# New order and new engines for the steps of a planned spectral-filter and ReGLU kernel

## The chip, the cores and the metric

The kernel runs on one core of one Trainium2 chip. The metric is the device time of one execution in microseconds (us), lower is better. A core has five engines that run their own instruction queues side by side: TensorE (PE, matrix products; PEld are its weight loads), VectorE (DVE), ScalarE (ACT), GpSimd (POOL) and SyncE (SP, which issues most DMAs).

## The reference

Everything is float32; x has 2048 rows of 512.

```python
def _A_ref(x, w_r, w_i):
    X = rfft2(x, axes=(-2, -1))
    return irfft2(X * (w_r + 1j * w_i), s=(S, D), axes=(-2, -1))

def _B_ref(x, W_gate, W_up, W_down):          # F = 1376
    gate = einsum("bsd,df->bsf", x, W_gate)
    up = einsum("bsd,df->bsf", x, W_up)
    gate = gate * (gate > 0)
    return einsum("bsf,fd->bsd", gate * up, W_down)

xn = _layernorm(x)
s = _A_ref(xn, A_w_r, A_w_i)
g = silu(_B_ref(xn, B_W_gate, B_W_up, B_W_down))
return x + s * g
```

## The kernel before

**The work.** The rows are held in eight chunks of 256 (two row tiles of 128) for the layernorm and the filter, and in four chunks of 512 (`c` = 0 to 3, four row tiles each) for the feed-forward part. All products are split into a high and a low float16 half and taken in three passes (high by high, high by low, low by high).

- *Filter.* The two-dimensional transform is done by matrix products. A first stage writes chunk after chunk to the DRAM buffer `A_d`. Then eight column groups `q` go through four PE stages each, `y`, `xx`, `z`, `v`, between which DVE and ACT build halves (`a`, `xsp`, `tt`, `pf`, `p`, `z`, `t`); the filter weights come in at `tt` (four products of 128x512 each group), and `pf` are their sums. The result goes to `C_d`. When all eight are there, a last stage per row chunk (`s`) gives `zz`, from which sums and differences `ae`, `ye` and `sv` are made; `sv` is the filtered signal.
- *Feed-forward.* For each row chunk and each of eleven feature tiles (ten of 128 and one, tile 10, of 96), `gu` are the gate and up products, `r` the rectified gate, `h` the product, in its float16 halves. `dn` is the down product, `g` its Silu. `rows_mw` is one small product that spreads a maximum over the partitions, from `wide_mw`, which DVE makes out of `mw`.
- *Nine pairs.* In row chunks 2 and 3, nine pairs of feature tiles (four in chunk 2, five in chunk 3) are computed by `fast_products` with seven block products of 12 matmuls instead of eight. The PE accumulates into three PSUM tiles `sa`, `sb`, `sc`; the other names are `sk` (a copy of `sc`), `se`, `sr`, `sq` and then two `h`. Such a pair needs sums of weight blocks: `rp` (four steps of 128x512 for a pair, one after the other), out of which `wT` and a part of `wgu` are made.
- *End.* `finish` multiplies `sv` by `g` (chunks before the last come back from the DRAM buffer `G_d`), adds x and stores. For some chunks x is copied to the output first and `sv` is added by a DMA that POOL issues; for the others DVE adds into `xt` and SP stores.

**What sets the order.** Nothing is issued when it is written. Each piece of work is a step with an engine, a cost, the tiles that it reads and writes, and a due time. `Plan.run` goes through all steps with a model of the five engines; each time it takes the step that can begin soonest, and among those that can begin equally soon the one that is due first. The planned start times give one list, and each engine executes its part of that list in this order; a helper records every instruction, so that all lines of the profile are its line, L197 (L206 after the change). `DUES` holds a due time for every step, and `WAITS` holds, for the steps that have one, how long before its due time a step may begin at the earliest:

```python
for s, due in zip(steps, DUES):
    s.due = due
for s, lead in zip([s for s in steps if s.lead is not None], WAITS):
    s.lead = lead
...
order.sort(key=lambda k: k[0])
for t, s in order:
    s.fn()
```

Other tables choose the engine of single steps: `NORMS` (normalising a row tile, DVE or ACT), `SUM2` (the sums `pf` or `tt`, two choices for each column group), `DIFF2` (the differences `ae`, two for each row chunk), `TSUMS` (the four `rp` steps of a pair), `SECONDS` (the product `se<-se,sq` of a pair) and `HLOWS` (the low half of a pair's `h`, two for each pair). `ROOM` holds the number of buffers of each kind; it is not changed, and for most `dn` tiles there is one PSUM buffer.

```python
eng, e, cost = (DVE, "DVE", dve(512)) if TSUMS[n] == "DVE" else (POOL, "POOL", pool(512))
e, eng, cost = (("DVE", DVE, dve), ("POOL", POOL, pool))[SECONDS[5 * c + n] == "POOL"]
e, eng, cost = (("DVE", DVE, dve), ("POOL", POOL, pool))[HLOWS[10 * c + 2 * n + m] == "POOL"]
```

Of the kernel before, what the change touches and what calls it, by code (L numbers as in the profile page):

```python
# [43 lines left out]
NORMS = ['DVE', 'DVE', 'DVE', 'DVE', 'DVE', 'ACT', 'ACT', 'DVE', 'DVE', 'DVE', 'ACT', 'DVE', 'DVE', 'ACT', 'DVE', 'DVE']  # L44
STATS, ADDS, COPIES = ['DVE', 'DVE', 'ACT', 'DVE', 'ACT', 'ACT', 'ACT', 'ACT'], ['DMA', 'DMA', 'DVE', 'DMA', 'DMA', 'DMA', 'DVE', 'DVE'], [105.83, 202.31, 0.24, 342.73, 748.16, 416.58, 501.03, 895.66]
# [9 lines left out]
SUM2, DIFF2 = ['DVE', 'DVE', 'DVE', 'POOL', 'POOL', 'DVE', 'DVE', 'POOL', 'DVE', 'POOL', 'DVE', 'POOL', 'DVE', 'POOL', 'DVE', 'POOL'], ['POOL', 'POOL', 'POOL', 'POOL', 'POOL', 'POOL', 'DVE', 'DVE', 'DVE', 'POOL', 'DVE', 'DVE', 'DVE', 'POOL', 'POOL', 'DVE']  # L55
ROOM = {"k4": 10, "k2": 8, "kg": 4, "cm": 3, "h16": 11, "xg": 3, "F": 2, "gu": 3, "dn": 1, "q": 4, "q4": 2, "mv": 4, "m": 4, "p": 4, "am": 1, "mid": 3}
CALM, SAFE, SAFE_LAG, RATE, TURNKB = 40, 1.0, 1.0, 320, 1300
SUMS, TSUMS, FMARGIN = ['DVE', 'DVE', 'DVE', 'DVE'], ['DVE', 'DVE', 'DVE', 'DVE', 'DVE'], 0.4
SECONDS, HLOWS = ['DVE', 'DVE', 'DVE', 'DVE', 'DVE', 'DVE', 'DVE', 'DVE', 'DVE', 'DVE', 'DVE', 'DVE', 'DVE', 'DVE', 'DVE', 'DVE', 'DVE', 'DVE', 'DVE', 'DVE'], ['DVE', 'DVE', 'DVE', 'DVE', 'DVE', 'DVE', 'DVE', 'DVE', 'DVE', 'DVE', 'DVE', 'DVE', 'DVE', 'DVE', 'DVE', 'DVE', 'DVE', 'DVE', 'DVE', 'DVE', 'DVE', 'DVE', 'DVE', 'DVE', 'DVE', 'DVE', 'DVE', 'DVE', 'DVE', 'DVE', 'DVE', 'DVE', 'DVE', 'DVE', 'DVE', 'DVE', 'DVE', 'DVE', 'DVE', 'DVE']
# [4 lines left out]
XDUE, SDUE = [-44.18, 1.62, 81.91, 105.7, 173.95, 99.44, 177.4, 146.02], [-114.62, 32.24, 147.09, 211.35]  # L64
DUES = (
    61.11, 143.08, 138.41, 136.86, 1e+09, 1e+09, 1e+09, 1e+09, 1e+09, 1e+09, 1e+09, 1e+09, 1e+09, 1e+09, 1e+09, 1e+09, 1e+09, 1e+09, 1e+09, 1e+09,
    1e+09, 1e+09, 1e+09, 1e+09, 1e+09, 1e+09, 1e+09, 1e+09, 1e+09, 1e+09, 1e+09, 1e+09, 1e+09, 1e+09, 1e+09, 1e+09, 1e+09, 1e+09, 1e+09, 1e+09, 1e+09,
    1e+09, 1e+09, 1e+09, 1e+09, 1e+09, -207.26, -219.43, -107.81, -43.91, -59.59, -32.12, -41.62, -126.94, -114.77, -112.31, -30.63, -43.52, -40.73,
# [1501 lines left out]
```

## Time and profile before

| | |
|---|---|
| median of 3 runs | 407.5 us (406.91 to 407.97) |
| the profiled execution | 408.49 us, its span 406.7 us |
| granted TensorE clock | 0.994 (1.00 from 170 to 400 us) |
| busy: PE, DVE, ACT, POOL | 391.2, 339.0, 245.4, 30.8 us |
| instructions on PE, DVE, ACT, POOL | 3332, 755, 478, 50 |
| first matmul, last matmul's end | 1.06 us, about 398.5 us |

The span runs from the first to the last instruction of the profiled execution; its own time is 1.8 us longer. PE's busy time counts a matmul as busy until the next one may follow, so a wait of PE shows as a gap between the starts of two matmuls and as an idle time in square brackets in the timeline, with what ended it. The other engines' idle time matters only where PE or the end waits for them.

### The profile page before, as it was taken

The numbers are of one execution on the slowest core, as the hardware profiler recorded it, in microseconds if no ns is written. First come the engines' busy times: TensorE is split into PE (matmuls) and PEld (weight loads), VectorE is DVE, ScalarE is ACT, GpSimd is POOL, SyncE is SP. The second block draws the span as 40 slices with busy tenths as digits, with TensorE's granted clock in tenths as the row PEclk, the third lists the DMA queues.
The fourth block names the chain that finished last, engine by engine and source line by source line (L and its number), as shares of the span: only waits on it lengthen the run. The fifth ranks groups of instructions, "written<-read, shape, count | busy, mean of one in ns | idle before, by whom it ended". The sixth has DMA issues, their size and how long they took to land.

```text
span 406.7 us, 8600 instructions
## 1 busy us (share of the span) xinstructions
PE 391.2 (96%) x3332; PEld 242.9 (60%) x3332; DVE 339.0 (83%) x755; ACT 245.4 (60%) x478; POOL 30.8 (8%) x50
## 2 busy tenths in 40 slices
PE   7999999999999999999999999999999999989991
PEld 5864444444444444455675776875567888866551
DVE  3899999899889995798787999998788853787993
ACT  5999976778376848664465983445354543662321
POOL 0000000000000000001001000100111000252311
PEclk9999999999999999999999999999999999999997
DMA  7974013049803997999475950545724059947786
GB/s 265 407 265 119 0 54 103 2 87 216 284 15 71 333 326 246 294 201 270 119 232 143 299 134 24 168 86 185 206 64 140 2 146 239 262 57 212 210 201 155
DMA packets 59353, 69.55 MB, mean 171 GB/s; under 512 B 24688, under 2 KB 36560, under 8 KB 59312
## 3 DMA queue, kind: packets, MB, share of 16 engines
q1 hardware_dynamic: 57872, 66.38, 56.1%
q0 software_dynamic: 1440, 2.62, 4.1%
q8 instruction: 26, 0.43, 0.4%
q14 instruction: 15, 0.12, 0.1%
HBM read 43.81 MB, written 22.56 MB: 163 GB/s over the span
## 4 chain that ended last, share of the span: by engine, by line
PE 59%; DVE 17%; DMA 12%; ACT 5%; issue 2%; SPq 2%; POOL 0%; DVEq 0%; ACTq 0%
PE dn L197 17%; PE gu L197 13%; PE sb L197 7%; PE sc L197 5%; PE sa L197 5%; DVE h L197 3%; DMA A_d<-t 3%; PE z L197 3%; PE xx L197 3%; DVE xs L197 2%; SPq L197 2%; PE y L197 2%; DVE t L197 2%; DMA x<-in_x 2%; DMA out<-sv 2%
## 5 line engine op out<-in xcount | busy, mean ns | idle before, releaser
L197 PEld LDWEIGHTS <-wgu 128*128 128x128 f16 x960 | 93.0, 98 | 64.8 <-issue 3.9
L197 PE MATMUL dn<-wds,h 128*128 128x512 f16 (+2 forms) x528 | 118.0, 373 | 1.4 <-ACT g L197 1.4
L197 PE MATMUL gu<-xT,wgu 128*128 128x512 f16 (+1 forms) x528 | 111.9, 369 | 0.4 <-DVE xT L197 0.4
L197 PEld LDWEIGHTS <-h 128*128 128x128 f16 (+1 forms) x594 | 53.8, 98 | 56.1 <-issue 4.6
L197 PEld LDWEIGHTS <-wT 128*128 128x128 f16 x324 | 31.3, 98 | 6.0 <-issue 0.5
L197 POOL TENSOR_TENSOR pf<-tt,tt 128x256 f32<-128x256 f32 x12 | 10.1, 846 | 264.2 <-ACT xsp L197 184.3
L197 PE MATMUL sa<-xT,wgu 128*128 128x256 f16 x216 | 26.6, 273 | 0.0
L197 PE MATMUL sb<-xS,wT 128*128 128x256 f16 x216 | 26.6, 273 | 0.0
L197 ACT ACTIVATE h<-h 128x512 f16<-128x512 f32 (+1 forms) x26 | 16.1, 624 | 15.4 <-DVE h L197 15.3
L197 DVE SCALAR_TENSOR_TENSOR tt<-xsp,cw,wt 128x512 f32<-128x512 f32 x32 | 23.2, 760 | 0.1
L197 DVE TENSOR_TENSOR h<-gu,r 128x512 f32<-128x512 f32 (+3 forms) x34 | 20.7, 608 | 1.8 <-ACT r L197 1.0
L197 ACT ACTIVATE r<-gu 128x512 f32<-128x512 f32 (+2 forms) x26 | 14.9, 574 | 10.8 <-PE gu L197 10.7
L197 DVE TENSOR_TENSOR h<-h,h 128x512 f16<-128x512 f32 (+1 forms) x26 | 17.6, 685 | 2.1 <-ACT h L197 2.0
L197 PE MATMUL gu<-xT,wgt 128*64 128x256 f16 (+1 forms) x144 | 17.1, 309 | 0.5 <-ACT r L197 0.4
L197 ACT ACTIVATE g<-dn,cdi 128x512 f32<-128x512 f32 (+1 forms) x16 | 10.7, 670 | 9.3 <-PE dn L197 5.2
L197 ACT ACTIVATE a<-y 128x1024 f16<-128x1024 f32 x8 | 8.1, 1018 | 12.1 <-PE y L197 11.0
L197 DVE SCALAR_TENSOR_TENSOR wgu<-raw,p,wgu 128x512 f16<-128x512 f32 x20 | 14.2, 746 | 0.1
L197 PE MATMUL sc<-xS,wgu 128*128 128x256 f16 x108 | 13.3, 273 | 0.9 <-DVE sr L197 0.9
L197 PEld LDWEIGHTS <-wgt 128*64 128x64 f16 (+1 forms) x144 | 9.6, 106 | 7.5 <-issue 1.9
L197 POOL TENSOR_TENSOR ae<-zz 128x126 f32<-128x126 f32 (+1 forms) x18 | 10.7, 722 | 40.7 <-issue 37.6
L197 ACT ACTIVATE rp<-rp,csc 128x512 f32<-128x512 f32 x20 | 13.4, 714 | 0.0
L197 PE MATMUL sc<-xT,wT 128*128 128x256 f16 x108 | 13.3, 273 | 0.0
(198 smaller groups left out, 666.2 us busy)
## 6 DMA issues: line engine op xcount, KB each, us to landing
A_d<-t SPq DMA_DIRECT2D x16, 256.0 KB, 4.0
rw<-in_wl SPq DMA_DIRECT2D x8, 512.0 KB, 4.4
wt<-in_wl SPq DMA_DIRECT2D x8, 512.0 KB, 4.9
at<-A_d SPq DMA_DIRECT2D x8, 512.0 KB, 5.3
C_d<-t SPq DMA_DIRECT2D x16, 256.0 KB, 3.5
ct<-C_d SPq DMA_DIRECT2D x16, 256.0 KB, 7.2
x<-in_x SPq DMA_DIRECT2D x7, 512.0 KB, 7.0
G_d<-g SPq DMA_DIRECT2D x12, 256.0 KB, 3.9
```

The lines of the kernel that those rows point to most:

```text
L197: return lambda *args, **kw: self.tc.keep_in_program_order(f(*args, **kw))
```

## The change

All of it is in the tables and in one planner cost. `DUES` and `WAITS` get new numbers, so every engine gets a new order. No instruction is added or taken away but those that two `NORMS` choices bring: PE has the same matmuls. The new choices of engine are:

- two normalisations (`xf<-x,mv,q`) go from DVE to ACT;
- twelve `rp` steps (three of the five pairs), four `se<-se,sq` and seven low halves of `h`, 23 steps of 128x512 in all, go from DVE to POOL;
- eighteen `ae` steps of 128x126 or 128x128 go from POOL to DVE;
- of the sixteen choices for `pf` and `tt` sums seven stay on POOL, but for other groups.

`DEVIATE` replaces a formula for the planner's cost of a DVE step by three constants; it changes no instruction.

```diff
-NORMS = ['DVE', 'DVE', 'DVE', 'DVE', 'DVE', 'ACT', 'ACT', 'DVE', 'DVE', 'DVE', 'ACT', 'DVE', 'DVE', 'ACT', 'DVE', 'DVE']
+NORMS = ['DVE', 'DVE', 'DVE', 'DVE', 'DVE', 'ACT', 'ACT', 'DVE', 'DVE', 'ACT', 'ACT', 'ACT', 'DVE', 'ACT', 'DVE', 'DVE']
-SUM2, DIFF2 = ['DVE', 'DVE', 'DVE', 'POOL', 'POOL', 'DVE', 'DVE', 'POOL', 'DVE', 'POOL', 'DVE', 'POOL', 'DVE', 'POOL', 'DVE', 'POOL'], ['POOL', 'POOL', 'POOL', 'POOL', 'POOL', 'POOL', 'DVE', 'DVE', 'DVE', 'POOL', 'DVE', 'DVE', 'DVE', 'POOL', 'POOL', 'DVE']
+SUM2, DIFF2 = ['DVE', 'POOL', 'DVE', 'POOL', 'DVE', 'POOL', 'DVE', 'POOL', 'POOL', 'DVE', 'POOL', 'DVE', 'DVE', 'POOL', 'DVE', 'DVE'], ['DVE', 'DVE', 'DVE', 'DVE', 'DVE', 'DVE', 'DVE', 'DVE', 'DVE', 'DVE', 'DVE', 'DVE', 'DVE', 'DVE', 'DVE', 'DVE']
-SUMS, TSUMS, FMARGIN = ['DVE', 'DVE', 'DVE', 'DVE'], ['DVE', 'DVE', 'DVE', 'DVE', 'DVE'], 0.4
+SUMS, TSUMS, FMARGIN = ['DVE', 'DVE', 'DVE', 'DVE'], ['POOL', 'DVE', 'POOL', 'POOL', 'DVE'], 0.4
-SECONDS, HLOWS = ['DVE', 'DVE', 'DVE', 'DVE', 'DVE', 'DVE', 'DVE', 'DVE', 'DVE', 'DVE', 'DVE', 'DVE', 'DVE', 'DVE', 'DVE', 'DVE', 'DVE', 'DVE', 'DVE', 'DVE'], ['DVE', 'DVE', 'DVE', 'DVE', 'DVE', 'DVE', 'DVE', 'DVE', 'DVE', 'DVE', 'DVE', 'DVE', 'DVE', 'DVE', 'DVE', 'DVE', 'DVE', 'DVE', 'DVE', 'DVE', 'DVE', 'DVE', 'DVE', 'DVE', 'DVE', 'DVE', 'DVE', 'DVE', 'DVE', 'DVE', 'DVE', 'DVE', 'DVE', 'DVE', 'DVE', 'DVE', 'DVE', 'DVE', 'DVE', 'DVE']
+SECONDS, HLOWS = ['DVE', 'DVE', 'DVE', 'DVE', 'DVE', 'DVE', 'DVE', 'DVE', 'DVE', 'DVE', 'POOL', 'DVE', 'DVE', 'DVE', 'POOL', 'POOL', 'DVE', 'POOL', 'DVE', 'DVE'], ['DVE', 'DVE', 'DVE', 'DVE', 'DVE', 'DVE', 'DVE', 'DVE', 'DVE', 'DVE', 'DVE', 'DVE', 'DVE', 'DVE', 'DVE', 'DVE', 'DVE', 'DVE', 'DVE', 'DVE', 'DVE', 'POOL', 'DVE', 'DVE', 'POOL', 'POOL', 'DVE', 'DVE', 'DVE', 'POOL', 'DVE', 'POOL', 'POOL', 'DVE', 'DVE', 'POOL', 'DVE', 'DVE', 'DVE', 'DVE']
+DEVIATE = (2.68, 2.54, 2.54)
 DUES = (
-    61.11, 143.08, 138.41, 136.86, 1e+09, 1e+09, 1e+09, 1e+09, 1e+09, 1e+09, 1e+09, 1e+09, 1e+09, 1e+09, 1e+09, 1e+09, 1e+09, 1e+09, 1e+09, 1e+09,
+    79.32, 134.5, 138.21, 132.46, 999999978, 999999983, 999999977, 999999984, 999999984, 999999985, 999999984, 999999986, 999999986, 999999987,
...
 )
 WAITS = (
-    44.14, 31.23, 11.27, 23.37, 40.49, 46.88, 145.21, 107.04, 0.1, 22.42, 110.28, 184.68, 43.83, 0.1, 5.2, 82.7, 116.95, 41.45, 22.26, 66.7, 104.78,
+    30.303362, 75.86468, 11.239413, 62.149805, 6.665444, 70.709887, 117.19794, 192.677905, 8.399014, 125.833056, 109.989298, 187.941761, 80.339107,
...
 )
...
-        step("DVE", 2.4 + .14 * sum("ACT" in NORMS[2 * c:2 * c + 2] for c in cs), run, reads=[(f"mv{c}", i) for c in cs for i in range(2 + (STATS[c] == "ACT"))], writes=[(name, 2)], port=True)
+        step("DVE", DEVIATE[cs[0] // 2 - 1], run, reads=[(f"mv{c}", i) for c in cs for i in range(2 + (STATS[c] == "ACT"))], writes=[(name, 2)], port=True)
```

**Where instructions move.** In the rows below the digits of a name are a piece or row tile and a buffer number; the row chunk's digit is cut off.

The first place is DVE around 172 us, where PE needs `wide_mw` for the small product `rows_mw`. `h_1_10` is tile 10's `h` of chunk 1. DVE before:

```order
L197 TENSOR_TENSOR h_1_10_2081<-gu_10_2020,r_10_2067 64x256 x2
L197 TENSOR_TENSOR h_1_10_2081<-gu_10_2020,r_10_2067 32x512
L197 TENSOR_TENSOR h_1_10_2096<-h_1_10_2081,h_1_10_2096 96x512
L197 COPY wt_1950<-spw 128x4 x2
L197 TENSOR_REDUCE mw<-mw 128x1
L197 TENSOR_SCALAR wide_mw<-unit,mw 128x128
```

DVE now, at the same place:

```order
L206 TENSOR_TENSOR sx_3_1_2035<-sx_1_1997,sx_3_1_2035 128x4x256
L206 COPY wt_1926<-spw 128x4 x2
L206 TENSOR_REDUCE mw<-mw 128x1
L206 TENSOR_SCALAR wide_mw<-unit,mw 128x128
L206 TENSOR_TENSOR h_1_10_2110<-gu_10_2041,r_10_2065 64x256 x2
L206 TENSOR_TENSOR h_1_10_2110<-gu_10_2041,r_10_2065 32x512
```

`wide_mw` now stands ahead of tile 10's `h` instead of behind its low half. On PE tile 10's products are parted: the 36 matmuls that stood together are now 12, then three `dn` of 3, and then the other 24 (the up product, 64 columns wide), which wait for ACT's `r`.

The second place is DVE around 220 us, where the pair 0 of chunk 2 ends (`sr_0`) and the sums of column group 2 (`pf`) are made. DVE before:

```order
L197 TENSOR_TENSOR t_0_2783<-v_2751,t_0_2783 128x2x512
L197 TENSOR_TENSOR wT_103<-rp_0_2124,wT_103 128x2x512
L197 TENSOR_TENSOR pf_2823<-tt_2_2749,tt_2_2743 128x8x32
L197 SCALAR_TENSOR_TENSOR tt_2_2826<-xsp_2735,cw,wt_2334 128x512
L197 TENSOR_TENSOR sr_0_2658<-sb_0_2553,sr_0_2658 128x512
L197 TENSOR_TENSOR pf_2823<-tt_2_2826,tt_2_2746 128x8x32
```

DVE now:

```order
L206 TENSOR_TENSOR z_0_2726<-z_2682,z_0_2726 128x1024
L206 SCALAR_TENSOR_TENSOR tt_2_2772<-xsp_2567,cw,wt_2336 128x512
L206 TENSOR_TENSOR tt_2_2772<-tt_2_2772,tt_2_2728 128x256
L206 TENSOR_TENSOR sr_0_2667<-sb_0_2545,sr_0_2667 128x512
L206 SCALAR_TENSOR_TENSOR tt_2_2809<-xsp_2567,cw,wt_2336 128x512
L206 TENSOR_TENSOR tt_2_2745<-tt_2_2745,tt_2_2809 128x256
```

And POOL now, from the sums of weights of one pair (`rp_0_2321`) to those of another (`rp_0_2634`); before, its only rows there were two sums `tt`:

```order
L206 TENSOR_TENSOR rp_0_2321<-rp_0_2321,rp_1_2132 128x512
L206 TENSOR_TENSOR se_0_2676<-se_0_2676,sq_0_2786 128x512
L206 TENSOR_TENSOR pf_2844<-tt_2_2772,tt_2_2728 128x8x32
L206 TENSOR_TENSOR pf_2844<-tt_2_2745,tt_2_2809 128x8x32
L206 TENSOR_TENSOR h_2_0_1_2884<-se_0_2676,h_2_0_1_2884 128x512
L206 TENSOR_TENSOR rp_0_2634<-rp_1_2670,rp_0_2634 128x512
L206 TENSOR_TENSOR rp_1_2670<-rp_1_2670 128x512
```

The sums `pf` are gone from DVE there, and POOL has become the queue in which weight sums, second products, `pf` and low halves of `h` stand behind one another.

The third place is PE around 364 us: the last three matmuls of `dn_2` of chunk 2, and the first of `dn_0` of chunk 3, which takes the same PSUM buffer after ACT has read it for `g`. PE before:

```order
L197 MATMUL dn_2_3886<-wds,h_2_10_3627 128x512
L197 LDWEIGHTS wT_105
L197 MATMUL sb_4_4920<-xS_2966,wT_105 128x256
...
L197 LDWEIGHTS h_3_0_0_4326
L197 MATMUL dn_0_5019<-wds,h_3_0_0_4326 128x512
```

PE now:

```order
L206 MATMUL dn_2_3802<-wds,h_2_10_3684 128x512
L206 LDWEIGHTS wgu_99
L206 MATMUL sb_3_4635<-xS_3019,wgu_99 128x256
...
L206 LDWEIGHTS wgu_100
L206 MATMUL sc_4_4886<-xS_3019,wgu_100 128x256
L206 LDWEIGHTS h_3_0_0_4321
L206 MATMUL dn_0_4905<-wds,h_3_0_0_4321 128x512
```

Before, twelve matmuls (one block product) stand between the two; now it is 36 (`sb`, `sa` and `sc`).

More of the change, by code (lines that the diff above doesn't have):

```diff
@@ L64 @@
 XDUE, SDUE = [-44.18, 1.62, 81.91, 105.7, 173.95, 99.44, 177.4, 146.02], [-114.62, 32.24, 147.09, 211.35]
+DEVIATE = (2.68, 2.54, 2.54)
 DUES = (
-    61.11, 143.08, 138.41, 136.86, 1e+09, 1e+09, 1e+09, 1e+09, 1e+09, 1e+09, 1e+09, 1e+09, 1e+09, 1e+09, 1e+09, 1e+09, 1e+09, 1e+09, 1e+09, 1e+09,
-    1e+09, 1e+09, 1e+09, 1e+09, 1e+09, 1e+09, 1e+09, 1e+09, 1e+09, 1e+09, 1e+09, 1e+09, 1e+09, 1e+09, 1e+09, 1e+09, 1e+09, 1e+09, 1e+09, 1e+09, 1e+09,
-    1e+09, 1e+09, 1e+09, 1e+09, 1e+09, -207.26, -219.43, -107.81, -43.91, -59.59, -32.12, -41.62, -126.94, -114.77, -112.31, -30.63, -43.52, -40.73,
[87 rows of a table removed]
+    79.32, 134.5, 138.21, 132.46, 999999978, 999999983, 999999977, 999999984, 999999984, 999999985, 999999984, 999999986, 999999986, 999999987,
+    999999986, 999999985, 1e+09, 999999989, 999999985, 999999990, 1.00000001e+09, 999999990, 999999994, 999999982, 999999992, 999999991, 999999993,
+    999999996, 999999994, 999999994, 999999975, 999999980, 999999996, 999999996, 999999996, 999999996, 1.00000003e+09, 1.00000004e+09, 999999992,
+    999999998, 999999997, 999999998, 999999999, 999999994, 999999998, 1e+09, -197.42, -228.87, -97.06, -69.59, -51.04, -40.78, -43.63, -76.9, -126.74,
[87 rows of a table added]
 )
 WAITS = (
[12 rows of a table removed]
[19 rows of a table added]
 )
```

203 rows, old and new, of tables (DUES, WAITS) are left out of this document.

## The prediction

> **What bounds the kernel now.** I read the page's parts first, then PE's waits, the 10-us windows, the groups by shape, and the timeline at each wait and at the end.
>
> ```profile
> PE 391.2 (96%) x3332; PEld 242.9 (60%) x3332; DVE 339.0 (83%) x755; ACT 245.4 (60%) x478; POOL 30.8 (8%) x50
> PE   7999999999999999999999999999999999989991
> DVE  3899999899889995798787999998788853787993
> ```
>
> PE is full in nearly every slice, and the change leaves its matmuls alone. So only three things can move the time: places where PE waits, the stretch after the last matmul, and new waits. PE's waits are few (columns: total us, times, longest):
>
> ```profile
> PE gu L197 <- ACT xTf L197: 1.7, 1, 1.7
> PE dn L197 <- ACT g L197: 1.4, 1, 1.4
> PE small L197 <- DVE md L197: 1.1, 1, 1.1
> PE rows_mw L197 <- DVE wide_mw L197: 1.0, 1, 1.0
> PE sc L197 <- DVE sr L197: 0.9, 1, 0.9
> PE gu L197 <- ACT r L197: 0.4, 1, 0.4
> PE gu L197 <- DVE xT L197: 0.4, 1, 0.4
> ```
>
> They sum to 6.9 us. `xTf`, `md` and `xT` belong to the start, whose PE order hardly differs now, and 0.4 for `r` stands between the same steps as before; these I leave. Three remain for the change: 1.4, 1.0 and 0.9, which is 3.3 us.
>
> **The three waits.** The first is at 172 us (start, length, engine, instruction; in brackets the idle time ahead of it):
>
> ```profile
> 172.38 0.69 DVE L197 TENSOR_TENSOR h<-h,h 96x512 f16<-96x512 f32 x1 [0.69 <-ACT h L197]
> 173.62 0.29 DVE L197 TENSOR_SCALAR wide_mw<-unit,mw 128x128 f32<-128x128 f32 x1
> 174.05 0.46 PE L197 MATMUL rows_mw<-wide_mw,ones 128*128 128x128 f32 x2 [0.99 <-DVE wide_mw L197]
> ```
>
> DVE made tile 10's low half, for which it idled 0.69 and worked 0.69, before `wide_mw`. Now `wide_mw` stands ahead of tile 10, and that cover of 1.38 us is larger than the wait of 0.99; PE also has one `dn` of three matmuls more between tile 10's last product and `rows_mw`. What can be late next is what ACT brings into `mw`, and the 24 parted matmuls of tile 10, which newly wait for ACT's `r`. Behind that wait all of PE's queue stands, and DVE's `h` of tile 10. The nearest row is the same pattern in chunk 0, where it costs 0.4 us. I credit 1.0 and debit nothing here; the ends are +0.6 and 0.
>
> The second is at 221 us:
>
> ```profile
> 218.25 2.75 PE L197 MATMUL gu<-xT,wgu 128*128 128x512 f16 x12
> 220.84 1.47 PE L197 MATMUL sa<-xT,wgu 128*128 128x256 f16 x12
> 221.50 0.42 DVE L197 TENSOR_TENSOR pf<-tt,tt 128x256 f32<-128x256 f32 x1 [2.35 <-DMA C_d<-t]
> 222.51 0.69 DVE L197 TENSOR_TENSOR sr<-sb,sr 128x512 f32<-128x512 f32 x1
> 223.25 1.47 PE L197 MATMUL sc<-xS,wgu 128*128 128x256 f16 x12 [0.94 <-DVE sr L197]
> 224.56 2.75 PE L197 MATMUL gu<-xT,wgt 128*128 128x512 f16 x12
> ```
>
> DVE stood 2.35 us in front of `pf` until the store of `t` freed its buffer, and `sr`, which frees the PSUM tile for `sc`, stood behind it in DVE's queue. Now POOL makes `pf`; DVE makes only the `tt` sums there, and the next thing behind `sr` does not hold PE. A wait for that buffer now holds POOL's queue: `se` is ahead of it, the low half of `h` and the next pair's four weight sums are behind it. By starts, twelve matmuls of 256 columns take 224.56 − 223.25 = 1.31 us and twelve of 512 take 220.84 − 218.25 = 2.59. The part of `v` that now stands between, in place of a `gu`, leaves `sr` about 1.5 us to spare by these rows. Credit 0.9.
>
> The third is at 364 us:
>
> ```profile
> 357.63 1.91 POOL L197 DMA_DIRECT2D out<-sv  x2 [1.51 <-DVE sv L197]
> 364.68 0.21 ACT L197 ACTIVATE ye<-zz 128x2 f32<-128x2 f32 x1 [1.94 <-DMA out<-sv]
> 364.79 0.67 ACT L197 ACTIVATE g<-dn,cdi 128x512 f32<-128x512 f32 x1
> 365.51 1.46 PE L197 MATMUL dn<-wds,h 128*128 128x512 f16 x6 [1.44 <-ACT g L197]
> ```
>
> `g` empties the one `dn` buffer, and it stood on ACT behind a two-column copy that waited 1.94 us for the DMA which POOL had issued out of `sv`. Now 36 matmuls (3 × 1.31 = 3.9 us) stand between the two `dn` instead of 12 (1.31), and the copy ahead of `g` waits for DVE's `ae` and no DMA. From rows like these I count `g` done some 2 us after the last `dn_2`, 1.9 ahead of need. Credit 1.4.
>
> **The steps that change engine.** These groups carry the prices (busy us, mean ns):
>
> ```profile
> L197 DVE TENSOR_TENSOR h<-h,h 128x512 f16<-128x512 f32 x22 | 14.9, 685 | 1.4 <-ACT h L197 1.3
> L197 DVE TENSOR_TENSOR ae<-zz 128x128 f32<-128x128 f32 x8 | 2.3, 315 | 0.0
> L197 DVE TENSOR_SCALAR xf<-x,mv,q 128x512 f32<-128x512 f32 x10 | 5.2, 541 | 0.0
> L197 DVE TENSOR_TENSOR p<-pf,p 128x1024 f16<-128x1024 f32 x8 | 10.3, 1288 | 3.3 <-ACT p L197 3.3
> L197 POOL TENSOR_TENSOR tt<-tt,tt 128x256 f32<-128x256 f32 x2 | 1.5, 726 | 31.1 <-DVE tt L197 24.6 <-issue 6.5
> L197 POOL TENSOR_TENSOR pf<-tt,tt 128x256 f32<-128x256 f32 x12 | 10.1, 846 | 264.2 <-ACT xsp L197 184.3
> L197 POOL TENSOR_TENSOR ae<-zz 128x128 f32<-128x128 f32 x8 | 5.7, 730 | 36.5 <-issue 33.4 <-ACT zz L197 3.1
> ```
>
> DVE loses 23 steps of 128x512, taken at the first row's 0.685, 15.8 us, and two normalisations of 0.541, 1.1 us; it gains 18 `ae` of about 0.3, 5.4 us. Net −11.5 of 339.0. This is worth nothing by itself where PE does not wait for DVE; it widens the cover. The two normalisations go to an ACT that is busy 245.4 of 406.7 us, early, where PE waits for neither engine.
>
> No POOL step of 512 elements is in the trace. Four `ae` in a row give one of 128, undisturbed:
>
> ```profile
> 344.90 1.64 POOL L197 TENSOR_TENSOR ae<-zz 128x128 f32<-128x128 f32 x4 [33.39 <-issue]
> ```
>
> 1.64 / 4 is 0.41, and 256 takes 0.726, so 128 elements more cost 0.32 and 512 come to 0.726 + 2 × 0.32 = 1.36. The bounds are twice the undisturbed 256 (1.45) and 1.2, should the fixed part be larger. With 1.36, 23 steps are 31.3 us; 18 `ae` (0.72 each) leave, 13 us. POOL goes from 30.8 to about 49 us, spread over 180 to 370 us, and stays an engine with room. [...]
>
> So each moved step takes twice as long, and a chain of four weight sums needs 5.4 us instead of 2.7. What hides it is distance: for pair 3 of chunk 2, for instance, PE has from the end of tile 10 to the first use of `wT` five block products (6.6), two of 512 columns (5.2) and some 2.7 of small stages, 14.5 us; ACT's two steps, POOL's four and ACT's `wT` need about 12. The other places that I counted leave 1.5 to 6 us; the tightest, 1.5, is the second `z` of group 0, whose `pf` stands on POOL behind weight sums.
>
> **Collisions.** A POOL step and a DVE step that both read SBUF stretch each other:
>
> ```profile
> 188.93 1.94 POOL L197 TENSOR_TENSOR pf<-tt,tt 128x256 f32<-128x256 f32 x2 [184.30 <-ACT xsp L197]
> 190.20 0.95 DVE L197 TENSOR_TENSOR tt<-tt,tt 128x256 f32<-128x256 f32 x1
> 310.51 0.43 DVE L197 TENSOR_TENSOR tt<-tt,tt 128x256 f32<-128x256 f32 x1
> 310.85 1.75 DVE L197 TENSOR_TENSOR p<-pf,p 128x1024 f16<-128x1024 f32 x1
> ```
>
> The `tt` took 0.95 instead of 0.43; the `p` took 1.75, and the other seven of its group (10.3 − 1.75) / 7 = 1.22. Beside the twelve `pf` and two `tt` on POOL I find eight such stretches, of which these are the first and the last, 2.9 us in all or 0.2 for each POOL step. For steps of 1.36 instead of the `pf`'s mean 0.846 I take 0.33, 7.6 us for 23. DVE's net gain shrinks from 11.5 to about 4, plus some 2 us that the `ae` on POOL stretched. It stays a gain.
>
> **The end.** PE's last matmul ended at about 398.5; then:
>
> ```profile
> 398.55 0.47 ACT L197 ACTIVATE g<-dn,cdi 128x256 f32<-128x256 f32 x1 [1.18 <-PE dn L197]
> 398.77 0.72 DVE L197 TENSOR_TENSOR sv<-sv,g 128x128 f32<-128x128 f32 x2
> 399.40 1.22 DVE L197 TENSOR_TENSOR xt<-xt,sv 128x128 f32<-128x128 f32 x3
> 399.71 1.45 SPq L197 DMA_DIRECT2D out<-xt  x3
> 380.00:390.00 10.00, 10.00 (x79) 5.15 (x72) 9.96 (x25) 4.41 (x14) 4.88 (x6) 1.00 0.97 264
> ```
>
> (The last row is a window: PE, PEld, DVE, ACT and POOL busy.) After `g` DVE still did five pieces, the last of 512 columns, and SP issued three stores. Now three small things follow the last matmul: `g`, one `sv` and one `xt` of 256 columns, and one store of 128 KB; POOL's last `out` is issued 33 matmuls ahead of the end. Two of the five pieces leave, 0.4 and 0.7; part of it returns if DVE still lags, since in 380 to 390 it is full. I take 0.7, with 0 and 1.5 as ends. The last `s` stage also comes earlier: by the order and these rates some 25 us of PE work ahead of the end instead of 18, which is the room for the 5.4 us of `ae` on DVE.
>
> **The sum.** 1.0 + 0.9 + 1.4 + 0.7 = 4.0 us. A new order will have new waits that I did not find; I allow one of the usual size, 0.9. Net −3.1: the profiled execution would go from 408.49 to 405.4, and the median, which lies 1.0 below it, from 407.5 to 404.4.
>
> **The rivals.**
>
> *POOL becomes what PE waits for* (slower). For: every moved step doubles, POOL is one queue in which `pf`, weight sums, `se` and low halves stand behind one another, and the collisions hit both sides. A chain of four is 2.7 longer, and with 0.5 for each collision 4.7; with slack of 1.5 to 3.5 it runs over by some 2.2. Where this happens at three places (a `z`, a `wT`, a low half in front of `dn`), PE loses 6.6, and 407.5 − 4.0 + 6.6 = 410.1. It decides from 4.0 us in total. Against: POOL idles most of the time, and `sr`, `se` and `sc`, which PE waits for directly, read one input from PSUM; none of the eight stretches is of such a step. [...]
>
> *The waits come back elsewhere* (no change). Three waits of about 1.1 in 400 us are what a planned order left before; three new ones give 407.5 − 4.0 + 3.3 = 406.8.
>
> *DVE holds the end* (no change). If the 5.4 us of `ae` meet a DVE that is as full as in 380 to 390, and only the 2.3 us of stretches leave, the end comes 3.1 later than PE allows: 407.5 − 3.3 + 3.1 = 407.3. Against: five of the 23 moved steps (3.4 us) lie there too.
>
> **How the numbers follow.** Forecast 0.53, POOL 0.29, waits elsewhere 0.11, DVE at the end 0.07. What a measurement can tell from no change is about 0.3%, 1.2 us. The forecast's own ends (tail 1.5, no new wait; no tail gain, one more wait) are 402.7 and 406.0; the range goes down to 402.3 for the runs' spread and up to 410.1 to take in the slower rival's middle. Of the forecast's 0.53 all but a little is faster, and a mild form of the rivals adds some: faster 0.55, same 0.16, slower 0.29.
>
> **What would show it.** PE's waits for `wide_mw`, `sr` and `g` gone from the list, POOL's 512-column steps near 1.36 us, DVE some 5 to 10 us less busy, fewer than three instructions after the last matmul on DVE. Wrong would be: PE waits on `z`, `wT` or a low half with POOL as the source, POOL steps of 1.7 us and more, DVE's two-input rows stretched as a group.

## The result and the profile after

The changed kernel takes 408.21 us in the median of 22 runs (404.9 to 409.04); the kernel before, run beside it, 408.0 (one of its 22 runs took 2314 us; without it the median is 407.97). The ratio is 0.9996, interval 0.9978 to 1.0013: no change. The forecast was 404.4 and faster. The profiled execution after took 406.79 us, its span 404.8 (before 408.49 and 406.7).

The page after, busy time and slices:

```profile
PE 392.4 (97%) x3332; PEld 244.3 (60%) x3332; DVE 331.8 (82%) x748; ACT 247.6 (61%) x480; POOL 53.8 (13%) x56
PE   8999999999999999999999999999999999959994
...
DVE  4988999989979987689897879998599743859994
...
PEclk9999999999999999999999999999999999998998
```

The slices show it already. Before, PE's last slice was a 1; now it is a 4, so less is left after the last matmul. But slice 36, at 354 to 364 us, is a 5, and the clock of the slice behind it fell to 8. PE's waits after (total us, times, longest):

```profile
PE sb L206 <- ACT sb L206: 4.2, 1, 4.2
PE small L206 <- DVE md L206: 1.1, 1, 1.1
PE gu L206 <- ACT xTf L206: 0.8, 1, 0.8
PE gu L206 <- ACT r L206: 0.4, 1, 0.4
PE gu L206 <- DMA raw<-in_wu: 0.4, 1, 0.4
PE gu L206 <- DVE xT L206: 0.4, 1, 0.4
```

The waits for `wide_mw`, `sr` and `g` are gone, as forecast. A single new one of 4.2 us stands in their place. The timeline around it (start, length, engine, instruction, in brackets the idle time ahead and what ended it):

```profile
355.40 0.69 DVE L206 TENSOR_TENSOR sv<-sv,g_3l 128x512 f32<-128x512 f32 x1
...
356.40 0.87 POOL L206 DMA_DIRECT2D out<-sv  x1 [0.54 <-DVE sv L206]
...
362.51 1.11 ACT L206 ACTIVATE zz<-s,cwi 128x1024 f32<-128x1024 f32 x1 [5.16 <-DMA out<-sv]
...
363.62 0.59 ACT L206 ACTIVATE sb<-sa 128x512 f32<-128x512 f32 x1
363.66 0.90 DVE L206 TENSOR_TENSOR ae<-zz 128x128 f32<-128x128 f32 x4 [4.50 <-ACT zz L206]
...
364.26 2.23 PE L206 MATMUL sb<-xS,wT 128*128 128x256 f16 x12 [4.20 <-ACT sb L206]
```

Read it from below. PE's products are added on top of a pair's PSUM tile `sb`, into which ACT first copies `sa` (`sb<-sa`). The copy had its data long before, but stands in ACT's queue behind `zz`, which ACT could not start for 5.16 us. `zz` (row chunk 0) was given the buffer (of kind `k4`, of which there are ten) in which `sv` of row chunk 1 had lain, and POOL's adding DMA was still reading that `sv`. The chain of waits gives that DMA its price:

```profile
356.09 0.31 DVE sr L206
356.40 6.00 DMA out<-sv
362.41 0.02 issue
```

Six microseconds from issue to landing. The plan did not underrate it: it has 1.2 for the issue, 1.6 for 512 KB at 320 KB per us and a lag of 3, which is 5.8. Nor is it a stray: over the kernel's DMAs out of `sv`, the view of that tile gives

```profile
DMA to landing us min/median/max: 4.4/5.5/6.9
```

DVE stood too, 4.50 us, in front of `ae<-zz`. And the twelve matmuls behind the wait took 2.23 us, where twelve of 256 columns took 1.47 before. Windows of 1 us show why (PE, PEld, DVE, ACT and POOL busy, then the granted clock and the DMA share):

```profile
361.00:362.00 1.00, 0.00 (x0) 0.00 (x0) 0.00 (x0) 0.00 (x0) 0.00 (x0) 1.00 1.09 348
...
364.00:365.00 1.00, 0.74 (x6) 0.62 (x6) 1.00 (x5) 0.61 (x5) 0.00 (x0) 0.90 0.07 12
365.00:366.00 1.00, 1.00 (x6) 0.75 (x5) 1.00 (x4) 0.00 (x0) 0.00 (x0) 0.50 0.05 6
366.00:367.00 1.00, 1.00 (x7) 0.69 (x6) 0.69 (x2) 0.00 (x0) 0.00 (x0) 0.50 0.73 225
367.00:368.00 1.00, 1.00 (x7) 0.69 (x6) 1.00 (x3) 0.00 (x0) 0.00 (x0) 0.50 0.08 31
368.00:369.00 1.00, 1.00 (x8) 0.67 (x7) 1.00 (x3) 0.25 (x1) 0.00 (x0) 0.89 0.00 0
```

From 364.8 to 368.2, for 3.4 us, the clock was 0.50. What is missing to 1.00 sums to 0.10 + 3 × 0.50 + 0.11 = 1.7 us. In the profiled execution before, no matmul after one of its waits (1.4, 1.0, 0.9) ran so. The wait cost 4.2 + 1.7 = 5.9 us in this execution.

The end after:

```profile
394.95 1.75 POOL L206 DMA_DIRECT2D out<-sv  x2 [9.16 <-DMA xt<-in_x]
...
395.65 5.77 SPq L206 DMA_DIRECT2D out<-xt  x6
395.86 3.77 PE L206 MATMUL dn<-wds,h 128*128 128x256 f16 x33
...
400.17 0.43 DVE L206 TENSOR_TENSOR sv<-sv,g 128x256 f32<-128x256 f32 x1 [2.01 <-ACT g L206]
400.63 0.43 DVE L206 TENSOR_TENSOR xt<-xt,sv 128x256 f32<-128x256 f32 x1
```

PE ends at 395.86 + 3.77 = 399.6 and the span at 404.8: a tail of 5.2 us, where before it was 406.7 − 398.5 = 8.2. The tail gives 3.0.

**The account** of the two profiled executions: PE's listed waits +0.2 (7.1 before, with 0.2 for `raw`; 7.3 after, with 0.4 each for `raw` and `xT`), clock +1.7, tail −3.0: −1.1, against −1.9 measured. The other −0.8 lies in gaps below what the list shows, and I did not trace it.

The profiled execution lies 1.4 us below the median. Its mean clock is 0.993; 14 of the 22 runs have 0.988 to 0.990. A step of 0.004 in the mean over 405 us is 1.6 us, about that difference. If the missing clock lies behind the wait in them too, the typical run loses some 3.3 us there, not 1.7; that is an estimate, since only one execution has its windows, and filling the wait (below) won back only 1.8.

### The profile page after: what moved, and what is told of

Its sections match the earlier page's. It is cut to its first block, busy times and chain, and to the rows that moved or that the text cites. A ratio compares the mean times of both kernels' runs of the same rounds, so it can differ in the third digit from the quotient of the medians.

```text
span 404.8 us, 8584 instructions
## 1 busy us (share of the span) xinstructions
PE 392.4 (97%) x3332; PEld 244.3 (60%) x3332; DVE 331.8 (82%) x748; ACT 247.6 (61%) x480; POOL 53.8 (13%) x56
## 4 chain that ended last, share of the span: by engine, by line
PE 84%; DMA 9%; DVE 3%; ACT 1%; SPq 1%; issue 1%; POOL 0%; ACTq 0%
PE gu L206 30%; PE dn L206 25%; PE sb L206 7%; PE sa L206 5%; PE sc L206 5%; PE z L206 3%; DMA g_2l<-G_d 3%; PE xx L206 3%; DMA ct<-C_d 2%; PE y L206 2%; DMA raw<-in_wu 2%; PE s L206 2%; PE v L206 2%; DMA out<-sv 1%; SPq L206 1%; DMA A_d<-t 1%
## 5 line engine op out<-in xcount | busy, mean ns | idle before, releaser
L206 POOL TENSOR_TENSOR rp<-rp,rp 128x512 f32<-128x512 f32 x9 | 12.4, 1372 | 169.6 <-ACT rp L206 169.2
L206 PE MATMUL sa<-xT,wgu 128*128 128x256 f16 x216 | 27.5, 279 | 0.0
L206 POOL DMA_DIRECT2D out<-sv x10 | 8.9, 1047 | 46.4 <-issue 15.8
L206 POOL TENSOR_TENSOR pf<-tt,tt 128x256 f32<-128x256 f32 x10 | 8.7, 880 | 40.6 <-DVE tt L206 21.2
L206 DVE TENSOR_TENSOR t<-v,t 128x1024 f16<-128x1024 f32 x8 | 9.8, 1222 | 4.7 <-ACT t L206 4.6
```

Of the source, the lines that this page charges most:

```text
L206: return lambda *args, **kw: self.tc.keep_in_program_order(f(*args, **kw))
```

## The experiments

Theory A: the time went into this one wait, which comes from the buffer that `zz` was given; without it the change is worth what the credits say. Rival B: removing the cause only lets the next thing behind the same DMA come to the front. Rival C: the clock behind a wait costs nothing of its own. Rival D: the new engines of the steps, not the order, brought what was gained. Each was timed with the kernel before beside it, so that the experiments are best compared by their ratios.

### Only the copy is moved ahead of `zz`

```diff
         order.sort(key=lambda k: k[0])
+        at = {s.order: i for i, (t, s) in enumerate(order)}
+        order.insert(at[1450], order.pop(at[1111]))
```

> Only ACT's order differs from the changed kernel: the copy of sa into sb for the last pair of chunk 3 is issued ahead of zz of row chunk 0, which waits for the adding DMA out of sv. Theory A (one new wait took the gain: PE's 4.2 us for this copy, and about 1.7 us of lowered TensorE clock behind it): PE's wait for the copy goes, the clock stays at 1.00 from 360 to 370 us, time 408.2 - 5.9 = 402.3, between 401.5 and 403.5 (ratio to before about 0.986). Theory B (zz itself is what the end needs; PE only waits elsewhere): 405.5 to 407.5. Theory C (the gain is lost to many small stretches by POOL's longer steps): 407 to 408.5.

407.06 us (405.46 to 409.33), ratio 0.9968, interval 0.9943 to 0.9992. The 402.3 is refuted; the time lies in the range of the expectation's theory B. The timeline of its profiled execution (405.46, the lowest of twelve):

```profile
362.87 1.11 ACT L206 ACTIVATE zz<-s,cwi 128x1024 f32<-128x1024 f32 x1 [5.07 <-PE sa L206]
...
364.01 0.90 DVE L206 TENSOR_TENSOR ae<-zz 128x128 f32<-128x128 f32 x4 [4.89 <-ACT zz L206]
...
366.50 0.69 DVE L206 TENSOR_TENSOR sc<-sb,sk 128x512 f32<-128x512 f32 x1
...
367.24 1.47 PE L206 MATMUL sb<-xS,wT 128*128 128x256 f16 x12 [3.78 <-DVE sc L206]
```

`zz` still starts at 362.87. ACT's queue no longer holds PE there, but DVE's does: `sc`, which must have read `sb` before PE adds to it again, stands behind `ae<-zz`. The view puts the idle time in front of `zz` down to a product `sa` that ended just then; `zz` reads nothing of it, and its own source, `s`, had ended at 357.5. It was the DMA out of `sv` again: issued at 356.36, it needed 6.4 us to landing, which is 362.8. So rival B holds for this remedy.

### `zz`, `ye` and one `sv` get storage of their own

The row chunk's `zz` and `ye`, and the `sv` of row chunk 2, are placed in the storage of weight sums that no one reads any more. The order is that of the change.

```diff
+        def own(n, k, a, b):
+            T.tile(n, "k4", lambda: wT[k].bitcast(F32)...[:, 0:a * b]...)
+        if c == 0:
+            own(zn, 0, 2, D)
+            T.tile(yen, "k4", lambda: wT[2].bitcast(F32)...[:, 0:1032]...)
+        if c == 2:
+            own(sn, 1, 2, D)
```

> The order is that of the changed kernel; zz and ye of row chunk 0 and sv of row chunk 2 are put into the storage of weight sums that are no longer used, so that zz need not wait until the adding DMAs have read sv of row chunk 1. Theory A: the wait of zz for the DMA goes and with it PE's wait; 401.5 to 403.5, as when the copy is issued ahead. If the wait only moves on to the next tile that takes the buffer (sv of row chunk 0, behind which the rest of ACT stands): 404 to 407. Theory C: 407 to 408.5.

**401.65 us** (400.63 to 401.88), ratio 0.9838, interval 0.9806 to 0.9871: it beats both kernels. PE's waits are now those of the start (total us, times, longest):

```profile
PE small L206 <- DVE md L206: 1.1, 1, 1.1
PE gu L206 <- ACT xTf L206: 1.0, 1, 1.0
PE small L206 <- ACT wgu L206: 0.6, 1, 0.6
PE gu L206 <- DVE xT L206: 0.4, 1, 0.4
PE gu L206 <- ACT r L206: 0.3, 1, 0.3
PE gu L206 <- DMA raw<-in_wu: 0.2, 1, 0.2
```

Its timeline has `zz`, under the name of the storage, 5.6 us earlier:

```profile
356.87 1.11 ACT L206 ACTIVATE wT<-s,cwi 128x1024 f32<-128x1024 f32 x1 [0.29 <-PE s L206]
```

Against the profiled execution after, its own is 5.1 shorter (401.68). The terms: wait −4.2, clock −1.7, tail +0.8 (PE ends at 393.7, the span at 399.7: 6.0), listed waits of the start +0.5 (3.6 against 3.1). They sum to −4.6; 0.5 is left over. Theory A holds, in place and in size, and rival B falls once the cause itself is gone.

### The wait is filled with work

16 products of zeros, 512 columns each, are added to a `dn` in front of the waiting `sb`; they change no value and take 3.6 us of the idle time.

```diff
+            if s.order in self.ahead:
+                self.ahead[s.order]()
             s.fn()
...
+    zeros = wT[0][:, 0, 0, 0, 0:P]
+    def fill():
+        for _ in range(16):
+            matmul(T["dn3_0"], zeros, wds[:, 0, 0, :], start=False, stop=False, skip_group_check=True)
+    T.ahead = {1086: lambda: POOL.memset(zeros, 0.0), 1114: fill}
```

> The changed kernel with 16 more matmuls of 512 columns (16 x 0.215 = 3.4 us), with a weight tile of zeros, into the running down product just ahead of the block product for which PE waits 4.2 us; POOL makes the zeros earlier. They lie inside the wait. If the lowered clock after the wait is a cost of its own: PE's idle time falls to about 0.8 us, the clock stays at 1.00, time 408.2 - 1.7 = 406.5 (405.8 to 407.2). If it costs nothing: 408.2. If the wait is often shorter than 3.4 us: 408.5 to 410.

406.42 us (405.56 to 407.31), ratio 0.9956, interval 0.9936 to 0.9976. Windows of 5 us:

```profile
360.00:365.00 5.00, 3.52 (x17) 1.46 (x16) 0.00 (x0) 0.88 (x1) 0.45 (x1) 1.00 0.87 213
365.00:370.00 5.00, 4.13 (x35) 3.42 (x35) 4.73 (x14) 2.42 (x10) 0.00 (x0) 1.00 0.19 55
```

The clock stays at 1.00 and no run's mean falls below 0.994. The DMA took 7.72 us in this profiled execution instead of 6.00, so `sb` was even later (365.87), PE still idled 2.35 us, and this one execution took 407.14 against 406.79. The gain is in the medians: 408.21 − 406.42 = 1.8, or 1.6 by the two ratios, whose intervals just miss each other. Nothing else that PE waits for was removed, so rival C falls: the clock has a price of its own, about this 1.8.

### The same remedy for the wait of before

Only `ye` of row chunk 0 in the kernel before is placed in a dead weight sum; that copy was what `g` stood behind at 364 us.

```diff
+        if c == 0:
+            T.tile(yen, "k4", lambda: wT[0].bitcast(F32)...[:, 0:1032]...)
```

> The kernel before, in its own order, with ye of row chunk 0 in the storage of weight sums that are no longer used, so that ACT's copy into ye does not wait for the adding DMAs out of sv of row chunk 1. If the prediction's third wait (PE 1.4 us for g) came from this buffer: that wait goes, 408.0 - 1.4 = 406.6 (406 to 407.2). If the end is held by the last DMAs whatever PE does: 407.5 to 408.2.

406.55 us (405.57 to 409.33), ratio 0.9957, interval 0.9935 to 0.998, that is −1.8, and PE's wait for `g` leaves its list. The order before had the same fault in small: 1.4 us of it. In the new order the same kind of wait is three times as long.

The profiled execution, at 409.33 the highest of the twelve, shows something else. PE stood 1.9 us for `wide_mw` instead of 1.0, and from 176.2 to 179.6 us, for 3.4 us, the clock was 0.50: the 8 in the eighteenth slice.

```profile
PE rows_mw L197 <- DVE wide_mw L197: 1.9, 1, 1.9
PEclk9999999999999999989999999999999999999997
```

So here the clock fell behind a wait of half the 4.2 us, and the mean clock of this execution is 0.988.

### The 24 sum steps back on DVE

Order and storage of the 401.65 kernel, with the old `TSUMS`, `SECONDS` and `HLOWS`; the order is written out as a list, so that the planner makes no other. The steps are 24 and not 23: DVE has 24 instructions more here than in the 401.65 kernel (772 against 748), POOL 24 fewer (32 against 56), and the rows of POOL after the change have five `se<-se,sq`, where `SECONDS` names four. The code shows why:

```python
e, eng, cost = (...)[SECONDS[5 * c + n] == "POOL"]
step(e, cost(512), lambda: eng.tensor_mul(T[E], T[E], T[r2]), ...)
for m, h32 in enumerate((r1, E)):
    ...
    e, eng, cost = (...)[HLOWS[10 * c + 2 * n + m] == "POOL"]
```

The lambda looks up `eng` only when the step is issued, and by then the loop has set it anew. So the product runs on the engine of the pair's second low half; for one pair the plan has it on DVE and POOL runs it.

```diff
-SUMS, TSUMS, FMARGIN = [...], ['POOL', 'DVE', 'POOL', 'POOL', 'DVE'], 0.4
+SUMS, TSUMS, FMARGIN = [...], ['DVE', 'DVE', 'DVE', 'DVE', 'DVE'], 0.4
...
```

> The changed kernel's order, step for step, with the storage of the second experiment; the 23 steps of 128x512 (weight sums, second products, low halves) are back on DVE at their places in the order, where each takes 0.69 us instead of 1.2 to 1.4 on POOL. If moving them is worth nothing by itself (DVE has room): 401.0 to 402.2, as in the second experiment. If DVE needed the 15.8 us between 170 and 340 us, where its windows are 80 to 100% full: PE waits for DVE there again, 403 to 406, with POOL at about 30 us busy.

401.79 us (401.56 to 402.17), ratio 0.9846, interval 0.9825 to 0.9868. The 24 steps on POOL are worth nothing, though DVE has 7.3 us more to do (338.9 instead of 331.6) with them back:

```profile
PE 390.3 (97%) x3332; PEld 243.1 (61%) x3332; DVE 338.9 (85%) x772; ACT 247.7 (62%) x480; POOL 21.5 (5%) x32
```

### The eighteen differences back on POOL

The same kernel with the old `DIFF2`; then only the four steps of the two row chunks that come last, and only the other fourteen.

```diff
-SUM2, DIFF2 = [...], ['DVE', 'DVE', 'DVE', 'DVE', 'DVE', 'DVE', 'DVE', 'DVE', 'DVE', 'DVE', ...]
+SUM2, DIFF2 = [...], ['POOL', 'POOL', 'POOL', 'POOL', 'POOL', 'POOL', 'DVE', 'DVE', 'DVE', 'POOL', 'DVE', 'DVE', 'DVE', 'POOL', 'POOL', 'DVE']
```

> The changed kernel's order, with the storage of the second experiment; eighteen ae steps are back on POOL as in the kernel before (the nine choices of the old table). If the move of ae to DVE pays (no collisions with DVE, no ae behind POOL's DMA issues): 402.5 to 404.5 here, DVE steps of two SBUF inputs stretched between 340 and 390 us. If it is worth nothing: 401.2 to 402.2. If DVE was what held the end: 400.5 to 401.2.

404.29 us (403.71 to 405.46), ratio 0.9908, interval 0.9886 to 0.9929, clear of the 401.65 kernel's (0.9806 to 0.9871). This move of engines is worth 2.6 us, and two runs ask where.

> Order and storage of the kernel with its own storage (401.65); only the last four differences, those of the two row chunks whose s stage comes last (around 374 to 383 us), are put back on POOL, where all eighteen cost 2.6 us. Theory L (the cost lies at the end, where DVE is full and the sum ye has to wait for a POOL step of 0.6 to 0.9 us): most of the 2.6 is here, 403.3 to 404.3 us, and the tail after the last matmul is longer than 5.1 us by about 1. Theory E (the cost lies in the PE wait on sc at 364 us and in the jitter of the start): 401.4 to 402.2 us and an unchanged tail.

402.87 us (402.39 to 404.07), ratio 0.9862, interval 0.9845 to 0.9879.

> The complement: the fourteen differences of the row chunks before the last two are put back on POOL, the last four stay on DVE. Theory L: 401.6 to 402.6 us, with the PE wait on sc of about 0.6 us still there. Theory E: 403.3 to 404.3 us.

403.74 us (402.7 to 404.69), ratio 0.9877, interval 0.9858 to 0.9896. By the ratios the last four cost 0.24% (1.0 us) and the other fourteen 0.39% (1.6 us): together the 2.6. Theory E's range holds for the fourteen and neither theory's for the last four; each thought that one place would carry nearly all. The split is rough, since either interval overlaps that of the 401.65 kernel, but the profiled executions show both places. With the fourteen on POOL, these are in PE's list:

```profile
PE sb L266 <- DVE sc L266: 1.4, 1, 1.4
PE small L266 <- DVE md L266: 1.1, 1, 1.1
PE dn L266 <- ACT g L266: 0.9, 1, 0.9
```

1.4 + 0.9 = 2.3 us that the 401.65 kernel does not have (with all eighteen on POOL the wait for `sc` was 0.6 in its profile, so the size varies); its tail is 5.4 instead of 6.0. With the last four on POOL no such wait appears, PE ends at 393.9 (393.7 there), and the tail is 400.9 − 393.9 = 7.0:

```profile
390.16 3.77 PE L266 MATMUL dn<-wds,h 128*128 128x256 f16 x33
...
393.97 0.47 ACT L266 ACTIVATE g<-dn,cdi 128x256 f32<-128x256 f32 x1 [3.24 <-PE dn L266]
394.48 0.42 DVE L266 TENSOR_TENSOR sv<-sv,g 128x256 f32<-128x256 f32 x1 [0.50 <-ACT g L266]
394.94 0.42 DVE L266 TENSOR_TENSOR xt<-xt,sv 128x256 f32<-128x256 f32 x1
```

DVE stood idle only 0.50 us ahead of its last `sv`, where in the 401.65 kernel it was 1.59. It still meets `g` in time, but what it feeds before that comes later: SP's six stores begin at 391.59, in the 401.65 kernel at 390.28, with PE at the same place within 0.2. That these late stores hold the end was not tried by itself. Rival D holds in part: of the change's two large moves of engines one is worth nothing and one 2.6 us, under an order that was planned for it.

### The kernel before without its last adding DMAs

The last two adding DMAs of row chunk 5, which POOL issues at 397.8 to 399.5 us, are left out; the output of these two row tiles lacks `sv·g`.

```diff
         for t, s in order:
-            s.fn()
+            if s.order not in (1644, 1648):
+                s.fn()
```

> The kernel before without the last two adding DMAs that POOL issues (the two row tiles of row chunk 5 keep x alone, so that part of the output is left out); all else is issued as before. If these DMAs, issued at 397.8 to 399.5 us with 6 us to land, hold the end of the kernel before: 408.0 - 1.5 to 2.5 = 405.5 to 406.5. If the last three stores of SP (issued to 400.8) hold it: 407.5 to 408.3.

405.95 us (404.62 to 406.61), ratio 0.993, interval 0.99 to 0.9959: −2.9, or −2.3 by the medians (408.23 beside it). Without them the tail is 404.1 − 398.5 = 5.6 us instead of 8.2, by this row of its timeline and its span:

```profile
396.74 1.80 PE L197 MATMUL dn<-wds,h 128*128 128x256 f16 x15
```

So these two held the end of the kernel before. The five DVE pieces and three stores that the prediction looked at would have let it end 2.6 us earlier. Part of the price of the two is that they slow the stores beside them: SP's 128 KB store needed 4.7 us from issue to landing before and 1.8 without them. Which of them landed last was not separated.

## Why the prediction was wrong

- **The three waits: right.** PE's list has none of them any more, neither after the change nor in the 401.65 kernel, where no later wait could hide them. That is the 3.3 us of the credits.
- **"A new order will have new waits that I did not find; I allow one of the usual size, 0.9": this step failed.** One new wait came, and it was 4.2, and with the clock 5.9 us in the profiled execution. With the measured sizes in place of its terms the sum is 3.3 + 3.0 − 5.9 = 0.4 us of gain instead of 3.1. The size was taken from the waits that an earlier order had left, but the length of a wait is set by the event that ends it, here a landing 6.0 us after its issue, whatever was left elsewhere. The plan did not foresee it either. As I read the code, the planner lets a step take whichever buffer of its kind comes free first, while the program hands buffers out in the order of the list; that this is why was not tested.
- **The same cause stood in the third wait.** There the prediction saw ACT's copy wait for the DMA out of `sv` and asked only whether `g` is now free of it. It did not ask which steps in the new order write into a buffer that such a DMA still reads. It was `ye` of row chunk 0 that took this buffer in the order before, and `zz` in the new one.
- **The clock: not in the sum at all.** After the idle 4.2 us it was 0.50 for 3.4 us, a loss of 1.7. The length of the idle time does not decide this alone: in the kernel with the moved copy PE idled 3.78 us and the profiled clock stayed at 1.00, and in the kernel before with `ye` in its own storage an idle 1.92 us was followed by 3.4 us at 0.50. What else decides it was not tested. In the kernel before, the waits of 1.4, 1.0 and 0.9 had a clock of 1.00 behind them. A wait of 0.9 and the one of 4.2 thus differed by more than their lengths.
- **The end: mis-sized.** 0.7 was forecast, 3.0 measured. It was counted on DVE's pieces. What held the end before were two adding DMAs issued about when PE ended, with the stores beside them. The prediction noted that the last ones are now issued 33 matmuls ahead, and gave it no price.
- **What the order is worth without the wait.** 6.6 us (ratio 0.9838), not the 4.0 of the credits. In the profiled executions the listed waits give 3.5 of it (7.1 to 3.6) and the tail 2.2 (8.2 to 6.0); the rest was not traced.
- **The steps on other engines.** POOL's price of 1.36 meets the mean of the float32 steps (below), but in part by luck: it was worked out for a step by itself, and such a step takes 1.27 (the median of the five `se<-se,sq`, of which the longest, stretched, took 1.62). That 24 and not 23 steps moved makes 0.7 us of DVE work and changes no rival. "Worth nothing by itself" was right for the sums. It was wrong for the differences, which it carried in the same net of DVE time: 2.6 us, because PE and, as it seems, the end wait for what follows them.
- **The rivals.** POOL as what PE waits for did not come: no wait of PE names it. "The waits come back elsewhere" (406.8) was nearest in kind, but it had three small waits and it was one large one. "DVE holds the end" (407.3) was nearer in time, for a reason that did not come: the tail became 3.0 shorter.

```profile
L206 POOL TENSOR_TENSOR rp<-rp,rp 128x512 f32<-128x512 f32 x9 | 12.4, 1372 | 169.6 <-ACT rp L206 169.2
...
L206 POOL TENSOR_TENSOR se<-se,sq 128x512 f32<-128x512 f32 x5 | 6.9, 1373 | 47.5 <-ACT sq L206 47.5
L206 POOL TENSOR_TENSOR h<-se,h 128x512 f16<-128x512 f32 x5 | 5.9, 1176 | 7.0 <-ACT h L206 6.2 <-DVE sr L206 0.7
```

These are the groups by shape after (busy us, mean ns, idle before). The float32 steps take 1.37 in the mean, the float16 ones 1.18. DVE's busy time fell by 7.2 us, inside the 5 to 10 that was named.

## What to carry to other kernels

When an order changes, look for each write into a buffer that a transfer may still read, and ask what stands behind it in that engine's queue: moving one step out of the queue only hands the wait to the next queue. Price a new wait by the event it ends on, not by the size of the old waits, and allow for a long PE wait costing more than its length: of the four longest that were profiled here, those of 1.92 and 4.20 us were followed by a lowered clock, those of 2.35 and 3.78 were not. At the end of a kernel, look first for what was issued last and lands latest.

## What the runs showed of the hardware

- After PE had idled 4.2 us its granted clock was 0.50 for 3.4 us, a loss of 1.7, and the same 3.4 us at 0.50 followed an idle 1.92 us in the kernel before with `ye` in its own storage. It stayed at 1.00 after an idle 3.78 and 2.35 us in two other executions. Keeping PE busy with zeros through most of the 4.2 us wait won 1.8 us in the median.
- The same adding DMA of POOL needed 6.00, 6.4 and 7.72 us from issue to landing in three executions, in the first beside DMA engines that were full (share 1.09 in the window at 361).
- Beside two such DMAs a 128 KB store of SP needed 4.7 us from issue to landing, without them 1.8.
- A POOL step of 128x512 with two float32 inputs took 1.37 us in the mean with a float32 output (1.27 in the median of `se<-se,sq`) and 1.18 with a float16 one (`h<-se,h`).
